# An explicit engine order for the QKV stage of a layernorm, linear-attention and SwiGLU kernel, with its weight sums moved to a later place

## The chip, the cores and the metric

The kernel runs on one core of one Trainium2 chip. Times are device microseconds (us) of one execution. The kernel was timed several times on the same chip beside the kernel that it is compared with; medians are given with the lowest and highest run. All runs used here are of the same (fast) state. The profile of a kernel is one execution, taken by the hardware profiler; its span is about 2 us shorter than the device time of the same execution.

Short names: PE is TensorE's matmul array, VectorE (DVE in the profile), ScalarE (ACT), GpSimd (POOL), SP the queue that issues most DMAs. The tiles in which the kernel collects PE's results (q_ps, kv_ps, nd_ps and others) are declared in PSUM, all its other tiles on the core in SBUF. L139 means line 139 of the kernel that is shown.

## The reference, cut to what matters

The input x is 2048 tokens by 1024. One normalized copy xn feeds a linear-attention block and a SwiGLU feed-forward, and the two results are combined.

```python
def phi(t): return where(t > 0, t + 1, exp(t)) + 1e-6
xn = layernorm(x)
q, k, v = split_heads(xn @ wqkv)          # 32 heads of 32
pq, pk = phi(q), phi(k)
kv  = einsum("bhsd,bhse->bhde", pk, v)    # sums over all 2048 tokens
z   = einsum("bhsd->bhd", pk)
num = einsum("bhqd,bhde->bhqe", pq, kv)
den = einsum("bhqd,bhd->bhq", pq, z)[..., None] + 1e-6
s   = (num / den) @ wo
g   = silu((silu(xn @ w_gate) * (xn @ w_up)) @ w_down)
out = x + s * g
```

Two consequences matter. The numerator (called ND below) needs kv of all tokens, so the kernel first runs k and v for all 16 token tiles (the QKV stage), then Q for a block of 512 tokens, then ND for that block. And the feed-forward is computed with a Winograd-like scheme on 2x2 blocks, for which sums of weight blocks (T1 to T4) are prepared on GpSimd while attention is still running.

## The kernel before

These are the parts that the change and the argument touch. Cuts are marked with "# ...".

The activation phi has two forms. Both are two VectorE steps after ScalarE's exponential; they differ in where the first step reads and writes:

```python
def emit_phi(work, t_ps, dst, W, in_place=False):
    e_t = work.tile([P, W], FP32, name="e_t", tag="e_t")
    ex = nc.scalar.activation(out=e_t[:], in_=t_ps, func=ACT.Exp)
    if in_place:                                   # first step stays in PSUM
        r = t_ps
        nc.vector.tensor_scalar(out=r, in0=t_ps, scalar1=0.0, scalar2=EPS, op0=ALU.max, op1=ALU.add)
    else:                                          # ScalarE copies to SBUF, first step SBUF to SBUF
        r_t = work.tile([P, W], FP32, name="r_t", tag="r_t")
        r = r_t[:]
        nc.scalar.activation(out=r, in_=t_ps, func=ACT.Relu)
        nc.vector.tensor_scalar(out=r, in0=r, scalar1=EPS, scalar2=None, op0=ALU.add)
    nc.vector.scalar_tensor_tensor(out=dst, in0=e_t[:], scalar=1.0, in1=r, op0=ALU.min, op1=ALU.add)
    return ex

def emit_Q(b, g):
    # ... eight matmuls into q_ps ...
    emit_phi(phiw, q_ps[:], pqT[:, g, :], TB)      # Q: the SBUF form, in both kernels
```

The weight sums: one set is four GpSimd sums and two DMA issues, also on GpSimd. prep takes the next of 14 sets from a queue: it loads a weight tile on SP and makes the sums.

```python
def emit_T(key, w):
    # ...
    nc.gpsimd.tensor_tensor(out=T1, in0=b12, in1=b11, op=ALU.subtract)
    nc.gpsimd.tensor_tensor(out=T2, in0=b22, in1=T1, op=ALU.subtract)
    nc.gpsimd.tensor_tensor(out=T3, in0=b22, in1=b12, op=ALU.subtract)
    nc.gpsimd.tensor_tensor(out=T4, in0=b21, in1=T2, op=ALU.subtract)
    # ... two nc.gpsimd.dma_start(...) that store T1..T4 in device memory

def prep(n, after=None):
    # ... t = w_slot(); load_gu(t, key[1], key[2], after); emit_T(key, t)
```

The QKV loop. The scheduler decides the order on each engine; the layernorm's Newton steps (reciprocal root by iteration), the norms and the copies of transposes are all VectorE's:

```python
for i in range(NT):                        # 16 token tiles
    ex = emit_B(i, 0)                      # k (c = 0, 1) and v (c = 2, 3) matmuls, phi in place
    # ...
    if i > 0:
        emit_C(i - 1)                      # kvz: pk^T [v, 1] of the tile before
    for c in range(1, NCH):
        if c == NCH // 2 and i + 2 >= TPB:
            stats_upto(i + 7)
        emit_B(i, c)
    if i >= 2 * TPB and i % 2 == 0:
        prep(1)                            # weight sums at tiles 8, 10, 12, 14
    nxt = i + 2
    if nxt < NPE:
        # ... emit_rstd (Newton steps) and emit_A2(nxt): norm, transposes, copy
    # ... for tiles 8 to 15: emit_rstd of four tiles, emit_A2_block: four norms (xn_blk),
    #     written to device memory on SP and read back transposed
# ...
gate(wq_loads, marks.get(("B", min(3, NT - 1))), sync=True)   # wq, wo: held until tile 3, tile 5
gate(wo_loads, marks.get(("B", min(5, NT - 1))), sync=True)
for g in range(G):
    emit_Q(0, g)
    if g % 4 == 3:
        prep(1)
```

The transposed attention output o of a block goes through device memory at once (emit_OT), and in the feed-forward the step c22 of the next key came after the matmuls and the evacuation of the present one:

```python
def emit_OT(b):
    # ...
    nc.sync.dma_start(out=blk_rows_pt(o_dram, b), in_=o_blk[:])
    nc.sync.dma_start_transpose(out=oT_tiles[b][:], in_=blk_rows(o_dram, b))
# ... feed-forward, for every key i:
    if i + 1 < n:
        emit_a(keys[i + 1])
    emit_b(keys[i])
    emit_evac(keys[i], h)
    if i + 1 < n:
        emit_c22(keys[i + 1])
```

Of the kernel before, what the change touches and what calls it, by code (L numbers as in the profile page):

```python
# [21 lines left out]
def kernel(  # L22
# [223 lines left out]
    with ExitStack() as p1:  # L246
# [5 lines left out]

        NXP = (NT + 1) // 2
# [32 lines left out]
        for i in range(nx, NT):  # L286
            load_x(i)
        wq_loads = [nc.gpsimd.dma_start(out=wq_sb[:, :, c * CW:(c + 1) * CW], in_=wqkv_v[:, :, c * CW:(c + 1) * CW])
                    for c in range(NCC)]
        wo_loads = [nc.gpsimd.dma_start(out=wo_sb[:, :, c * CW:(c + 1) * CW], in_=wo_v[:, :, c * CW:(c + 1) * CW])  # L290
                    for c in range(NCC)]

# [9 lines left out]
        def grp_of(i):  # L302
            return i if i < TPB else TPB - 1 + i // TPB

        def grp_tiles(gid):
            if gid < TPB:
                return [gid]
            b = gid - TPB + 1
            return list(range(b * TPB, min((b + 1) * TPB, NT)))

        def emit_stats(i):
            gid = grp_of(i)
            if gid not in grp_state:
                mv = small.tile([P, TPB, AGG], FP32, name="mv", tag="mv")
                rstd = small.tile([P, TPB], FP32, name="rstd", tag="rstd")
                grp_state[gid] = (mv, rstd, grp_tiles(gid))
            mv, rstd, tiles = grp_state[gid]
            k = tiles.index(i)
            stats = small.tile([P, NSC, nc.vector.BN_STATS_DIM], FP32, name="stats", tag="stats")
            xr = x_ap(i).rearrange("p (c f) -> p c f", f=SCH)  # L320
            sts = [nc.vector.bn_stats(out=stats[:, c, :], in_=xr[:, c, :]) for c in range(NSC)]  # L321
            if TPB <= i < 2 * TPB:
                late_gates.append((sts, ("B", min(1, NT - 1))))
            nc.vector.bn_aggr(out=mv[:, k, :], in_=stats[:])
            ln_state[i] = (mv, rstd, k)
            return sts
# [13 lines left out]
        def emit_rstd(gid):  # L340
            mv, rstd, tiles = grp_state[gid]
            n = len(tiles)
            a = small.tile([P, TPB], FP32, name="lna", tag="lna")
            nc.vector.tensor_scalar(out=a[:, 0:n], in0=mv[:, 0:n, 1], scalar1=EPS_LN, scalar2=None, op0=ALU.add)
# [5 lines left out]
            for _ in range(NR_ITERS):  # L350
                if n == 1:
                    nc.vector.scalar_tensor_tensor(out=w[:, 0:1], in0=y, scalar=a[:, 0:1], in1=y,
                                                   op0=ALU.mult, op1=ALU.mult)
                else:
                    nc.vector.tensor_tensor(out=w[:, 0:n], in0=y, in1=y, op=ALU.mult)
                    nc.vector.tensor_tensor(out=w[:, 0:n], in0=w[:, 0:n], in1=a[:, 0:n], op=ALU.mult)
                nc.vector.tensor_scalar(out=w[:, 0:n], in0=w[:, 0:n], scalar1=-0.5, scalar2=1.5,
                                        op0=ALU.mult, op1=ALU.add)
                nc.vector.tensor_tensor(out=y, in0=y, in1=w[:, 0:n], op=ALU.mult)
# [7 lines left out]
        def emit_A2(i):  # L367
            tok = slice(i * P, (i + 1) * P)
            xn = work.tile([P, D], BF16, name="xn", tag="xn")
            tr_ps = psC.tile([P, DC, P], BF16, name="tr_ps", tag="C")  # L370
            nh = 2 if (i == 0 and DC % 2 == 0) else 1
            dch = DC // nh
            cp = None
            for hh in range(nh):
                cols = slice(hh * dch * P, (hh + 1) * dch * P)
                emit_norm(i, xn[:, cols], cols=(cols if nh > 1 else None))
                for dc in range(hh * dch, (hh + 1) * dch):
                    nc.tensor.transpose(tr_ps[:, dc, :], xn[:, dc * P:(dc + 1) * P], ident[:])
                cp = nc.vector.tensor_copy(out=xn_ap(slice(hh * dch, (hh + 1) * dch), tok),
                                           in_=tr_ps[:, hh * dch:(hh + 1) * dch, :])  # L380
            ln_state.pop(i)
            return cp
# [11 lines left out]
        def emit_B(i, c):  # L394
            tok = slice(i * P, (i + 1) * P)
            if i not in pkv_tiles:
                pk_sb = work.tile([P, D], BF16, name="pk_sb", tag="pk_sb")
                pkv_tiles[i] = (pk_sb, v_bufs[i % 2])
            pk_sb, v_sb = pkv_tiles[i]
            kv_ps = psB.tile([P, CW], FP32, name="kv_ps", tag="B")  # L400
            for dc in range(DC):
                mm = nc.tensor.matmul(kv_ps[:], lhsT=xn_ap(dc, tok), rhs=wkv_sb[:, dc, c * CW:(c + 1) * CW],  # L402
                                      start=(dc == 0), stop=(dc == DC - 1))
                if dc == 0 and c == 0:
                    marks[("B", i)] = mm
            if c < NCC:
                return emit_phi(phiw, kv_ps[:], pk_sb[:, c * CW:(c + 1) * CW], CW, in_place=True)
            else:
                vc = c - NCC
                return nc.scalar.copy(out=v_sb[:, vc * GPC:(vc + 1) * GPC, 0:P],  # L410
                                      in_=kv_ps[:].rearrange("p (g c) -> p g c", c=P))
# [10 lines left out]
        nstat = 0  # L422

        def stats_upto(n):
            nonlocal nstat
            while nstat < min(n, NT):
                emit_stats(nstat)
                nstat += 1

        NPE = min(PE_T_BLOCKS * TPB, NT)  # L430
        cp0 = None
        sq_last = None
        for i in range(min(2, NT)):
            sts = emit_stats(i)
            nstat = i + 1
            if i > 0:
                gate(sts, cp0)
            sq_last = emit_rstd_act(grp_of(i))
            cp = emit_A2(i)
            if i == 0:  # L440
                cp0 = cp
        for i in range(NT):
            ex = emit_B(i, 0)
            if i == 0:
                gate([ex], sq_last)
            if i > 0:
                emit_C(i - 1)
            for c in range(1, NCH):
                if c == NCH // 2 and i + 2 >= TPB:
                    stats_upto(i + 7)  # L450
                emit_B(i, c)
            if i >= 2 * TPB and i % 2 == 0:
                prep(1)
            nxt = i + 2
            if nxt < NPE:
                if nxt < TPB:
                    stats_upto(nxt + 1)
                    emit_rstd(grp_of(nxt))
                elif nxt % TPB == 0:
                    stats_upto(nxt + TPB)  # L460
                    emit_rstd(grp_of(nxt))
                emit_A2(nxt)
            nb_ = (i + TPB) // TPB
            if (i + TPB) % TPB == 0 and nb_ >= PE_T_BLOCKS and nb_ < NB and i + TPB >= NPE:
                stats_upto((nb_ + 1) * TPB)
                emit_rstd(grp_of(nb_ * TPB))
                emit_A2_block(nb_)
        emit_C(NT - 1)
        gate([x_loads[i] for i in range(first_wave, NT)], marks.get(("B", min(1, NT - 1))), sync=True)
        for insts, key in late_gates:  # L470
            gate(insts, marks.get(key))
        gate(wq_loads, marks.get(("B", min(3, NT - 1))), sync=True)
        gate(wo_loads, marks.get(("B", min(5, NT - 1))), sync=True)
# [30 lines left out]
    with ExitStack() as p2:  # L504
# [36 lines left out]
        def emit_OT(b):  # L541
            oT_tiles[b] = otp.tile([P, G, TB], BF16, name="oT", tag="oT")
            o_blk = o_blks.pop(b)
            nc.sync.dma_start(out=blk_rows_pt(o_dram, b), in_=o_blk[:])
            nc.sync.dma_start_transpose(out=oT_tiles[b][:], in_=blk_rows(o_dram, b))
# [24 lines left out]
        for b in range(NB):  # L570
# [9 lines left out]
            for t in range(TPB):  # L580
                emit_ND(b, t)
                fill(1 if lastb else 2)
                if t % 2 == 1:
                    prep(1)
            emit_OT(b)
# [15 lines left out]
    with ExitStack() as p3:  # L601
# [35 lines left out]
        def emit_c22(key):  # L637
            p, kind, fg = key
            x_, zw, s2, s3, _ = grp[key]
            if kind == "g":  # L640
                c = xnp.tile([P, 4, TB], FP32, name="sg", tag="xn8")
                sg_tiles[(p, fg)] = c
            else:
                c = cp_.tile([P, 4, TB], FP32, name="cu", tag="cu")
            nc.vector.tensor_tensor(out=c[:, 3, :], in0=zw[:, 1, :], in1=s3[:], op=ALU.add)
            grp[key][4] = c

        def emit_b(key):
# [3 lines left out]
            x_, zw = grp[key][0:2]  # L652
            prod(zw[:, 0, :], lambda k: T4[:, k, :], lambda k: A22[:, k, :], False)
            prod(zw[:, 1, :], lambda k: w[:, HK + k, P:2 * P], lambda k: S4[:, k, :], False)
            prod(x_[:], lambda k: w[:, HK + k, 0:P], lambda k: x1[:, HK + k, :], False)

        def emit_evac(key, h):
            p, kind, fg = key
            x_, zw, s2, s3, c = grp.pop(key)
            nc.vector.tensor_tensor(out=c[:, 1:3, :], in0=zw[:], in1=s2[:, None, :].to_broadcast([P, 2, TB]),  # L660
                                    op=ALU.add)
            if kind == "g":
                nc.scalar.activation(out=c[:, 1:4, :], in_=c[:, 1:4, :], func=ACT.Silu)  # L663
# [9 lines left out]
        NRES = 5  # L673

        def emit_down(p, sw, h, w0, last):
# [17 lines left out]
            for q in range(NQ - NRES):  # L693
                load_w_to(w0 + q + 6)
                for t in range(TPB):
# [29 lines left out]
        with tc.manual_schedule(engines={mybir.EngineType.PE, mybir.EngineType.DVE, mybir.EngineType.Activation,  # L725
                                         mybir.EngineType.Pool}):
            base = 0
            for pi, p in enumerate(passes):
# [17 lines left out]
                for i in range(n):  # L746
# [5 lines left out]
                    emit_b(keys[i])  # L752
                    emit_evac(keys[i], h)
                    if i + 1 < n:
                        emit_c22(keys[i + 1])
# [38 lines left out]
```

## Time and profile before

| what | value | which view |
|---|---|---|
| time | 828.19 us (827.65 to 829.03, 3 runs) | runs |
| span, PE busy | 825.6 us, 96% | page, part 1 |
| PE idle before the first transpose | 6.2 us | PE waits |
| longest wait of PE inside the QKV stage | 8.9 us, for VectorE's pk | PE waits |
| last kvz matmul, first nd_ps, first yb (feed-forward) | 147.2, 164.1, 266.3 us | PE timeline |
| GpSimd's sums | 1.15 us each, 48.5 to 149.8 us | GpSimd timeline |

PE is busy 96% of the span, so only its idle stretches can be won. The page shows the span in 40 slices of 20.6 us; a digit is the busy share in tenths, and PEclk is the granted clock of TensorE in tenths of full speed:

```profile
PE   5976999999999999999999999999999999999997
...
PEclk9997999999999999999999999999999999999999
```

The third and fourth slices (41 to 83 us) have PE at 7 and 6, and the clock is at 7 in the fourth. The PE's waits (columns: total us, times, longest) name the cause:

```profile
PE kv_ps L402 <- DVE pk_sb L140: 8.9, 1, 8.9
PE tr_ps L378 <- DVE xn L364: 6.7, 3, 6.2
PE zw L613 <- DVE cu L645: 2.2, 2, 1.1
PE s_ps L555 <- DMA oT<-o_dram: 1.5, 1, 1.5
```

A kv matmul waits 8.9 us for pk, a VectorE result. (6.2 of the 6.7 us of the second line are the start.) The windows of the core show how busy the engines were; in each line: us, then busy us and instructions of PE, weight loads, VectorE, ScalarE and GpSimd, then clock and DMA:

```profile
40.00:60.00 20.00, 17.68 (x110) 8.96 (x108) 20.00 (x49) 5.36 (x10) 11.36 (x12) 1.00 0.64 205
60.00:80.00 20.00, 11.88 (x57) 5.73 (x57) 15.21 (x28) 2.37 (x4) 9.08 (x11) 0.74 1.06 323
...
140.00:160.00 20.00, 19.99 (x106) 9.47 (x104) 11.17 (x22) 9.75 (x18) 10.88 (x13) 1.00 0.50 200
160.00:180.00 20.00, 20.00 (x121) 10.19 (x120) 18.29 (x57) 11.08 (x21) 0.00 (x0) 1.00 0.00 1
```

VectorE is full from 40 to 60 us and PE loses 8 us of the next 20. Why VectorE is late is seen only in its timeline. VectorE first (start us, us, line, operation):

```profile
53.70 3.99 DVE L359 TENSOR_TENSOR rstd<-rstd,lnw 128x4 f32<-128x4 f32 x1
...
61.69 3.98 DVE L364 TENSOR_SCALAR xn_blk<-xp,mv,rstd 128x1024 bf16<-128x1024 bf16 x1
```

A step that multiplies 128x4 numbers, L359, takes 3.99 us (usual: 0.15), and a norm, L364, takes 3.98 us (usual: 0.54). GpSimd in the same stretch:

```profile
54.27 1.17 POOL L212 TENSOR_TENSOR T_1055<-w_sb 128x512 fp32r<-128x512 bf16 x1
55.39 1.15 POOL L214 TENSOR_TENSOR T_1056<-w_sb 128x512 fp32r<-128x512 bf16 x1
56.50 1.15 POOL L213 TENSOR_TENSOR T_1055<-w_sb,T_1055 128x512 fp32r<-128x512 bf16 x1
...
62.00 1.16 POOL L212 TENSOR_TENSOR T_1177<-w_sb 128x512 fp32r<-128x512 bf16 x1
```

L359 starts at 53.70, while GpSimd issues a DMA, and ends at 57.69, when the three sums from 54.27 on have ended (the last one at 57.65); the norm of 61.69 ends at 65.67, after the three sums that begin at 62.00. So the sums seem to hold VectorE.

Q's two VectorE steps of before; the sums ended at 149.8 us, just before the first of them:

```profile
149.89 0.43 DVE L139 TENSOR_SCALAR r_t<-r_t 128x512 f32<-128x512 f32 x1 [1.54 <-ACT r_t L138]
150.35 0.69 DVE L140 SCALAR_TENSOR_TENSOR pqT<-e_t,r_t 128x512 bf16<-128x512 f32 x1
...
152.08 0.69 DVE L140 SCALAR_TENSOR_TENSOR pqT<-e_t,r_t 128x512 bf16<-128x512 f32 x1
```

### The profile page before, as it was taken

What the parts mean: (1) busy time and instruction counts of PE and PEld (TensorE: products, weight loads), DVE (VectorE), ACT (ScalarE), POOL (GpSimd) and SP (SyncE); (2) the same over time, 40 slices, a digit from 0 to 9 for tenths busy, and PEclk for the clock granted to TensorE, in tenths of its full rate; (3) what the DMA queues carried; (4) which work ended last, traced back from release to release, by engine and by line L of the source; (5) the groups of instructions that cost most, each with busy time, mean ns of one, the idle gap of its engine ahead of it and who ended that gap; (6) DMA issues with size and microseconds to landing.
All of it is one profiled execution on the core that took longest, in us unless ns stands there. A gap on an engine that the chain in (4) does not pass through costs nothing.

```text
span 825.6 us, 9966 instructions
## 1 busy us (share of the span) xinstructions
PE 794.9 (96%) x3808; PEld 431.9 (52%) x3808; DVE 465.7 (56%) x787; ACT 202.9 (25%) x312; POOL 185.3 (22%) x221
## 2 busy tenths in 40 slices
PE   5976999999999999999999999999999999999997
PEld 2443444454454666666664444456666666544443
DVE  7996343695753666767665044166676676611305
ACT  2221333554533222122221021022212212200102
POOL 0064799300011253443650010010000000000100
PEclk9997999999999999999999999999999999999999
DMA  9469998217343678778687448389777777753641
GB/s 305 159 208 330 320 336 326 105 52 185 98 156 111 193 232 268 236 235 273 206 296 240 153 131 314 122 255 348 236 257 254 247 233 264 261 169 127 226 150 52
DMA packets 149566, 178.91 MB, mean 217 GB/s; under 512 B 30736, under 2 KB 105872, under 8 KB 149520
## 3 DMA queue, kind: packets, MB, share of 16 engines
q1 hardware_dynamic: 137792, 137.25, 52.0%
q0 software_dynamic: 11584, 40.90, 14.0%
q8 instruction: 30, 0.49, 0.2%
q10 hardware_dynamic: 144, 0.13, 0.0%
q14 instruction: 16, 0.13, 0.0%
HBM read 127.93 MB, written 44.04 MB: 208 GB/s over the span
## 4 chain that ended last, share of the span: by engine, by line
PE 88%; DVE 8%; DMA 3%; SPq 0%; issue 0%; ACT 0%; ACTq 0%
PE zw L613 24%; PE y_pd L690 12%; PE xb L613 11%; PE y_ps L690 11%; PE kv_ps L402 9%; PE q_ps L157 7%; PE s_ps L555 6%; PE yb L613 6%; DVE stats L321 2%; DMA xp<-in_A_x_dram 1%; PE nd_ps L527 1%; DVE xn_blk L364 1%; DVE kv_ps L134 1%; DMA oT<-o_dram 1%; DMA w_sb<-in_B_w_up_dram 1%; DMA w_sb<-in_B_w_down_dram 1%
## 5 line engine op out<-in xcount | busy, mean ns | idle before, releaser
L690 PEld LDWEIGHTS <-hT 128*128 128x128 bf16 x896 | 87.7, 98 | 107.3 <-issue 1.7
L402 PE MATMUL kv_ps<-wkv_sb,xnT 128*128 128x512 bf16 x512 | 117.8, 387 | 10.2 <-DVE pk_sb L140 8.9
L613 PE MATMUL xb<-xnT,w_sb 128*128 128x512 bf16 x448 | 115.5, 380 | 0.4 <-DMA w_sb<-in_B_w_up_dram 0.4
L690 PE MATMUL y_pd<-w_sb,hT 128*128 128x512 bf16 x448 | 103.2, 379 | 1.4 <-DMA w_sb<-in_B_w_down_dram 1.4
L690 PE MATMUL y_ps<-w_sb,hT 128*128 128x512 bf16 x448 | 103.2, 379 | 0.0
L720 DVE TENSOR_TENSOR sy<-sy,io 128x512 f32<-128x512 f32 (+1 forms) x33 | 22.2, 673 | 140.1 <-ACT sy L719 140.1
L613 PEld LDWEIGHTS <-w_sb 128*128 128x128 bf16 x672 | 56.8, 98 | 83.7 <-issue 30.2
L723 POOL DMA_DIRECT2D out_dram<-io x24 | 13.0, 543 | 337.8 <-DVE io L721 337.8
L402 PEld LDWEIGHTS <-xnT 128*128 128x128 bf16 x512 | 50.1, 100 | 68.3 <-issue 14.0
L663 ACT ACTIVATE sg<-sg 128x1536 f32<-128x1536 f32 x28 | 41.6, 1486 | 122.7 <-DVE sg L660 122.7
L555 PE MATMUL s_ps<-wo_sb,oT 128*128 128x512 bf16 x256 | 56.6, 379 | 1.5 <-DMA oT<-o_dram 1.5
L157 PE MATMUL q_ps<-xnT,wq_sb 128*128 128x512 bf16 x256 | 57.2, 379 | 0.0
L669 DVE TENSOR_TENSOR hT<-cu,sg 128x1536 bf16<-128x1536 f32 x28 | 49.9, 1781 | 0.0
L719 ACT ACTIVATE sy<-y_pd 128x512 f32<-128x512 f32 x16 | 8.7, 594 | 156.3 <-PE y_pd L690 156.3
L134 DVE TENSOR_SCALAR kv_ps<-kv_ps 128x512 f32<-128x512 f32 x32 | 22.3, 699 | 42.8 <-ACT e_t L131 42.7
L555 PEld LDWEIGHTS <-oT 128*128 128x128 bf16 x256 | 24.7, 98 | 30.6 <-DMA oT<-o_dram 2.0
L157 PEld LDWEIGHTS <-wq_sb 128*128 128x128 bf16 x256 | 24.6, 98 | 27.4
L560 POOL DMA_DIRECT2D s_dram<-s_sb x16 | 8.7, 543 | 108.5 <-ACT s_sb L557 108.5
L131 ACT ACTIVATE e_t<-kv_ps 128x512 f32<-128x512 f32 x32 | 19.1, 597 | 47.7 <-PE kv_ps L402 30.3
L613 PE MATMUL zw<-S_4505,w_sb 128*128 128x512 f16 x112 | 29.0, 382 | 0.0
L613 PE MATMUL zw<-S_2588,w_sb 128*128 128x512 f16 x112 | 29.0, 382 | 0.0
L557 ACT CAST s_sb<-s_ps 128x512 bf16<-128x512 f32 x32 | 18.8, 586 | 38.2 <-PE s_ps L555 37.6
(970 smaller groups left out, 1181.9 us busy)
## 6 DMA issues: line engine op xcount, KB each, us to landing
w_sb<-in_B_w_down_dram SPq DMA_DIRECT2D x56, 512.0 KB, 3.6
w_sb<-in_B_w_gate_dram SPq DMA_DIRECT2D x40, 512.0 KB, 4.8
w_sb<-in_B_w_up_dram SPq DMA_DIRECT2D x28, 512.0 KB, 6.1
o_dram<-o_blk SPq DMA_DIRECT2D x4, 1024.0 KB, 4.4
s_dram<-s_sb POOLq DMA_DIRECT2D x16, 256.0 KB, 2.7
io<-in_A_x_dram SPq DMA_DIRECT2D x16, 256.0 KB, 3.1
io<-s_dram SPq DMA_DIRECT2D x16, 256.0 KB, 3.4
xp<-in_A_x_dram SPq DMA_DIRECT2D x15, 256.0 KB, 6.4
```

The lines of the kernel that those rows point to most:

```text
L131: ex = nc.scalar.activation(out=e_t[:], in_=t_ps, func=ACT.Exp)
L134: nc.vector.tensor_scalar(out=r, in0=t_ps, scalar1=0.0, scalar2=EPS, op0=ALU.max, op1=ALU.add)
L157: nc.tensor.matmul(q_ps[:], lhsT=wq_sb[:, dc, g * P:(g + 1) * P], rhs=xn_ap(dc, btok), start=(dc == 0), stop=(dc == DC - 1))
L321: sts = [nc.vector.bn_stats(out=stats[:, c, :], in_=xr[:, c, :]) for c in range(NSC)]
L402: mm = nc.tensor.matmul(kv_ps[:], lhsT=xn_ap(dc, tok), rhs=wkv_sb[:, dc, c * CW:(c + 1) * CW], start=(dc == 0), stop=(dc == DC - 1))
L555: nc.tensor.matmul(s_ps[:], lhsT=oT[:, c, ttok], rhs=wo_sb[:, c, cc * CW:(cc + 1) * CW], start=(c == 0), stop=(c == G - 1))
L557: nc.scalar.copy(out=s_sb[:, cc * CW:(cc + 1) * CW], in_=s_ps[:])
L613: nc.tensor.matmul(out, lhsT=lhs(k), rhs=rhs(k), start=(first and k == 0), stop=(k == HK - 1), skip_group_check=True)
L663: nc.scalar.activation(out=c[:, 1:4, :], in_=c[:, 1:4, :], func=ACT.Silu)
L669: nc.vector.tensor_tensor(out=hv[:, TB:4 * TB], in0=c[:, 1:4, :].rearrange("p a b -> p (a b)"), in1=sg[:, 1:4, :].rearrange("p a b -> p (a ...
L690: nc.tensor.matmul(ys[(t, c)], lhsT=h[:, fc, tt], rhs=wt[:, o:o + CW], start=(fc == 0), stop=(fc == FC - 1), skip_group_check=True)
L720: nc.vector.tensor_tensor(out=sy[:], in0=sy[:], in1=s_in[:, cs], op=ALU.mult)
```

## The change

The intent is to remove the hole of PE in the QKV stage by taking work off VectorE and by moving the sums out of its way, and to remove some small waits later. In the QKV stage every engine's order is now written by hand: tiles 0 and 1 use each weight chunk together, layernorm runs two tiles ahead, the Newton steps go to GpSimd, the copies of the transposes go to ScalarE from tile 2 on, and sums are asked for only from tile 10 on. For tiles 0 to 8, k's phi takes the SBUF form. Later: o is transposed in halves, c22 (one VectorE add on a key's products) comes ahead of the matmuls of the present key, the SiLU is done in more, smaller steps, and the down projection begins with three weight tiles at once. The core of the diff:

```diff
+        p1_man = ExitStack()
+        p1_man.enter_context(tc.manual_schedule(engines={PE, DVE, Activation, Pool, SP}))   # cut
-        wq_loads = [nc.gpsimd.dma_start(...)]           # cut: gated until tile 3
-        wo_loads = [nc.gpsimd.dma_start(...)]           # cut: gated until tile 5
         def emit_rstd(gid):
+            eng = nc.gpsimd
-            nc.vector.tensor_scalar(out=a[:, 0:n], in0=mv[:, 0:n, 1], scalar1=EPS_LN, ...)
+            eng.tensor_scalar(out=a[:, 0:n], in0=mv[:, 0:n, 1], scalar1=EPS_LN, ...)
             for _ in range(NR_ITERS):
+                eng.tensor_tensor(out=w[:, 0:n], in0=y, in1=y, op=ALU.mult)
+                eng.tensor_tensor(out=w[:, 0:n], in0=w[:, 0:n], in1=a[:, 0:n], op=ALU.mult)
+                eng.tensor_scalar(out=w[:, 0:n], in0=w[:, 0:n], scalar1=-0.5, scalar2=1.5, ...)
+                eng.tensor_tensor(out=y, in0=y, in1=w[:, 0:n], op=ALU.mult)
# ... emit_TR: the copy of the transposes
+                if i < 2:
+                    nc.vector.tensor_copy(out=dst, in_=tr_ps[:])
+                else:
+                    nc.scalar.copy(out=dst, in_=tr_ps[:])
# ... emit_Bev
-                return emit_phi(phiw, kv_ps[:], pk_sb[:, c * CW:(c + 1) * CW], CW, in_place=True)
+                emit_phi(phiw, kv_ps[:], pk_sb[:, c * CW:(c + 1) * CW], CW, in_place=i >= 9)
# ... the order of tiles 0 and 1 by hand, then the loop:
+        for i in range(2, NT):
+            for c in range(NCH):
+                emit_Bmm(i, c)
+                # ... TR(i + 1), C(i - 1), Bev(i, c), N(i + 2), layernorm of i + 3
+            if i == 3 or i == 5:       # wq, wo loads: by program order in GpSimd's queue
+                # ... nc.gpsimd.dma_start(...)
+            if i >= 10:
                 prep(1)
# ... emit_OT(b, hf): half a block at a time; feed-forward:
                     if i + 1 < n:
                         emit_a(keys[i + 1])
-                    emit_b(keys[i])
+                        emit_c22(keys[i + 1])
+                    emit_b(keys[i], i == n - 1)
                     emit_evac(keys[i], h)
-                    if i + 1 < n:
-                        emit_c22(keys[i + 1])
# ... SiLU of c22 apart from the rest; NRES 5 -> 4; QF = 3 tiles of the down projection first
```

## The prediction

> **What bounds the kernel now.** PE is busy 96% of the 825.6 us span (page, busy table), so only PE's idle stretches can be won. The stretches and the table of waits show: 6.2 us before the first transpose; 8.9 us at 59-68 us, where a kv matmul waits for VectorE's pk; shorter waits of 0.4-0.8 us before and between; 1.5 us for the last transposed o; in the feed-forward stage 2.2+0.7 us of zw waiting for cu/sg and 1.8 us for weights; a 5 us tail. The QKV stage ends at 147.4 us, though its warm pace (7.37 us per tile, chain of waits) would need about 121 us. The 9 us hole also drops the granted clock to 0.5 (64-72 us).
>
> Why VectorE was late: it is 100% busy from 20 to 68 us (windows), and from 49 us GpSimd's weight sums (1.15 us each) hold it up: one rstd step took 3.99 us instead of 0.15, one norm 3.98 instead of 0.5, each ending with a run of three sums (timeline). [...]
>
> **What the change does in the QKV stage.** Newton steps (about 12 small operations per group, 0.15-0.2 us) go to GpSimd, transpose copies (0.68 us) to ScalarE; weight sums start only after the last block norm. Tiles 0 and 1 share weight chunks. I expect no PE hole over 2 us: first matmuls at the same 6-7 us, stage end near 132 us (7.7 + 16x7.37 + 7 transposes x 0.45[...]), so 13-16 us won.
>
> **What it costs: the main doubt.** In before, GpSimd's sums end at 149.8 us, just before the first Q evacuation. In after, the first weight load for a sum stands on the DMA queue behind the last block's transpose; I estimate the first sum at about 86 us. Fifteen sets at 5.65 us each (trace) end near 170 us, so 35 us of them fall on Q (from 132 us). Q's evacuation is r_t (0.43 us, SBUF to SBUF) and a two-input step on two SBUF tensors (0.69 us): both kinds collide. If VectorE passes only in the gaps between runs, it finishes one Q per about 5 us instead of 1.73. ND needs all eight, so PE then stalls up to 10-24 us.
>
> **Elsewhere.** Half-block o transposes remove the 1.5 us wait; c22 ahead of evacuation removes about 2.9 us of zw waits; NRES/QF up to 1 us: 4-5 us won.
>
> **Sum.** 828 - 15 (QKV) - 4.5 (elsewhere) + 16 (Q, between 2 and 24): 825 us, range 808-836. Within 2%, unless the collision is mild.
>
> **What would show it.** Right: windows 20-70 with PE full; granted clock 1.0 there; QKV ends 130-134 us; in the Q stretch r_t and pqT instructions of 2-5 us against 0.43/0.69, PE idle waiting for them until the sums end, and the first nd_ps later than 160 us (before: 164.1). Wrong: r_t stays at 0.43 us on average and first nd_ps near 148 us: then about 809 us.
>
> **What would make it wrong.** The sums run at another time; [...] small GpSimd Newton steps are much slower than on VectorE (0.2 us) and delay norms in tiles 2-7; VectorE falls behind.
>
> Chances: faster by over 2%: 0.2; within 2%: 0.76; slower by over 2%: 0.04.

Cut from it is a term of 2 us in the sum for the end of the QKV stage: with it the sum came to 130.8 us ("near 132"), the terms that remain give 128.8 us. What the trace of before shows is that the first 13 kv matmuls, from 7.72 us on, took 4.70 us and 11 of them from 13.64 us on 2.54 us, with the clock at 1.00 from 0 to 20 us; what slowed the first ones isn't shown. The "warm pace" is that of the undisturbed tiles of before, 7.37 us each (kv matmuls from 82.05, 89.42 and 96.79 us on), with the clock at 1.00. "Both kinds collide" rests on the two steps of before shown above: L359, with two SBUF inputs, took 3.99 instead of 0.15 us, and the norm L364, from SBUF to SBUF, 3.98 instead of 0.54 us.

## The result, and the profile after

The changed kernel took 829.65 us (829.32 to 830.66, 4 runs); before, on the same chip, took 828.07 us (827.65 to 829.03, 4 runs). The ratio is 1.002, with a 95% interval of 1.0002 to 1.0037: the same within 2%. Here and below a ratio is the mean time of one kernel's fast runs over the mean of the other's of the same rounds, so it is not quite the ratio of the medians that are quoted.

The same parts of the page for the changed kernel (slices of 20.7 us):

```profile
PE   6999999579999999999999999999999999999997
...
PEclk9999999769999999999999999999999999999999
```

The hole of the third and fourth slices is gone, and a new one is in the eighth and ninth (145 to 186 us), with the clock at 7 and 6. PE's waits:

```profile
PE q_ps L157 <- ACT r_t L138: 9.6, 4, 4.8
PE tr_ps L384 <- DVE xn L360: 8.4, 3, 6.0
PE nd_ps L552 <- DVE pqT L140: 5.3, 2, 2.8
PE kv_ps L408 <- DMA xnT<-xn_dram: 1.5, 1, 1.5
```

No wait for pk, cu, w_down or oT is left. In their place Q's matmuls wait 9.6 us for ScalarE's r_t, and ND waits 5.3 us for pqT. ScalarE is not the origin: it waits itself for VectorE's pqT, 26.0 us in eight times, because r_t and e_t have two buffers each. The windows:

```profile
40.00:60.00 20.00, 18.33 (x108) 9.22 (x109) 13.96 (x34) 9.11 (x15) 13.80 (x42) 1.00 0.35 114
60.00:80.00 20.00, 18.44 (x107) 9.23 (x110) 13.17 (x28) 9.50 (x17) 5.20 (x15) 1.00 0.96 255
...
140.00:160.00 20.00, 13.27 (x46) 5.11 (x46) 19.90 (x8) 4.34 (x8) 19.94 (x22) 0.77 0.84 291
160.00:180.00 20.00, 11.56 (x45) 4.88 (x44) 18.48 (x27) 6.12 (x12) 13.27 (x15) 0.63 0.60 234
```

PE wins 6.6 us in 60 to 80 us (18.44 against 11.88) and loses 6.7 and 8.4 us in the two windows after 140 us. VectorE is busy 19.90 of 20 us with only 8 instructions. Four of them in a row:

```profile
140.13 3.83 DVE L139 TENSOR_SCALAR r_t<-r_t 128x512 f32<-128x512 f32 x1
144.00 0.69 DVE L140 SCALAR_TENSOR_TENSOR pqT<-e_t,r_t 128x512 bf16<-128x512 f32 x1
144.61 6.03 DVE L139 TENSOR_SCALAR r_t<-r_t 128x512 f32<-128x512 f32 x1
150.67 0.69 DVE L140 SCALAR_TENSOR_TENSOR pqT<-e_t,r_t 128x512 bf16<-128x512 f32 x1
```

with GpSimd beside them:

```profile
142.52 1.15 POOL L215 TENSOR_TENSOR T_1899<-w_sb,T_1898 128x512 fp32r<-128x512 bf16 x1
143.62 0.57 POOL L220 DMA_DIRECT2D t_g_1904<-T_1898  x1
144.19 0.53 POOL L220 DMA_DIRECT2D t_g_1905<-T_1899  x1
144.75 1.17 POOL L212 TENSOR_TENSOR T_1910<-w_sb 128x512 fp32r<-128x512 bf16 x1
```

The r_t of 140.13 takes 3.83 us instead of 0.43 and ends at 143.96, after the last sum of a run of three; pqT then passes in 0.69 us inside the two DMA issues (143.62 to 144.72). The next r_t starts at 144.61, 0.14 us before the next sum, and is held for five sums, until 150.64. Only in the last set of sums (167.0 to 172.3 us) does VectorE pass after each sum, with steps of 1.4 to 1.6 us. There the second sum starts 0.08 us after the first has ended (168.24 after 168.16); in the runs of sums that held VectorE, each sum starts just within the end of the one before (by 0.03 to 0.06 us in the change). In the kept traces of all kernels, a waiting r_t, pqT or block norm passed at all five boundaries between two sums that have such a gap; of 83 boundaries without one it passed at 12, at 11 of them right after it had passed at the boundary before (in the change alone: at the one with a gap, and at 2 of 17 without, at 169.4 and 171.0 us). That fits the gap as what lets VectorE in, but no run tested it, and in before_late_sums VectorE also passed after each of five sums between 137.8 and 144.6 us, which leave no such gap. So, before the last set, one Q passes per set of DMA issues: from 139.53 to 166.25 the pqT steps begin 4.5 or 6.7 us apart, 5.3 us on average, where before took 1.73. Over the whole kernel the step L139 reads (min/median/max ns):

```profile
L139 DVE TENSOR_SCALAR r_t<-r_t x50: 374/427/6028, 14.2 to 233.9; 128x512 f32<-128x512 f32 x50
```

PE meanwhile:

```profile
166.30 0.99 PE L552 MATMUL nd_ps<-KVZ,pqT 128*128 128x132 bf16 x6
...
172.93 0.29 PE L552 MATMUL nd_ps<-KVZ,pqT 128*128 128x132 bf16 x1 [2.57 <-DVE pqT L140]
173.02 4.47 PE L157 MATMUL q_ps<-xnT,wq_sb 128*128 128x512 bf16 x10
```

The first nd_ps is issued at 166.30 but its group of eight is complete only at 172.93, when the sums have ended too (172.3 us).

Adding up the profiled spans (825.6 and 828.0): the last kvz matmul ends 12.2 us earlier (147.4 to 135.2). From there to Q's first matmul after the first ND group takes 37.8 us instead of 17.1 us: 20.7 us lost. From there to the first yb of the feed-forward it is 102.7 against 101.8 us: 0.9 us lost. The feed-forward from its first yb takes 552.3 instead of 559.3 us: 7.0 us won. The sum is -12.2 + 20.7 + 0.9 - 7.0 = +2.4 us, the difference of the spans. Everything that was won is given back in one place.

### The profile page after: what moved, and what is told of

Same layout as the page of the kernel before. It is cut to its first block, busy times and chain, and to the rows that moved or that the text cites. A ratio compares the mean times of both kernels' runs of the same rounds, so it can differ in the third digit from the quotient of the medians.

```text
span 828.0 us, 10023 instructions
## 1 busy us (share of the span) xinstructions
PE 794.4 (96%) x3736; PEld 434.3 (52%) x3808; DVE 475.1 (57%) x728; ACT 221.5 (27%) x364; POOL 214.4 (26%) x325
## 4 chain that ended last, share of the span: by engine, by line
PE 87%; DVE 7%; DMA 3%; POOL 2%; issue 1%; ACT 1%; DVEq 0%; ACTq 0%
PE zw L641 25%; PE xb L641 12%; PE y_pd L726 11%; PE y_ps L726 11%; PE kv_ps L408 9%; PE s_ps L583 7%; PE yb L641 6%; PE q_ps L157 5%; DVE r_t L139 3%; DMA xnT<-xn_dram 1%; DMA xn_dram<-xn_blk 1%; PE nd_ps L552 1%; DVE pqT L140 1%; DVE sy L763 0%; DVE stats L322 0%
## 5 line engine op out<-in xcount | busy, mean ns | idle before, releaser
L408 PE MATMUL kv_ps<-wkv_sb,xnT 128*128 128x512 bf16 x499 | 114.3, 383 | 2.1 <-DMA xnT<-xn_dram 1.5
L641 PE MATMUL xb<-xnT,w_sb 128*128 128x512 bf16 x420 | 113.7, 380 | 1.5
L157 PE MATMUL q_ps<-xnT,wq_sb 128*128 128x512 bf16 x250 | 64.2, 410 | 10.1 <-ACT r_t L138 9.6
L698 ACT ACTIVATE sg<-sg 128x1024 f32<-128x1024 f32 x28 | 29.6, 1058 | 97.1 <-DVE sg L694 97.1
L139 DVE TENSOR_SCALAR r_t<-r_t 128x512 f32<-128x512 f32 x50 | 46.0, 920 | 15.4 <-ACT r_t L138 15.1
L131 ACT ACTIVATE e_t<-q_ps 128x512 f32<-128x512 f32 x32 | 19.1, 597 | 50.2 <-DVE pqT L140 26.0
```

The lines of the kernel that those rows point to most:

```text
L157: nc.tensor.matmul(q_ps[:], lhsT=wq_sb[:, dc, g * P:(g + 1) * P], rhs=xn_ap(dc, btok), start=(dc == 0), stop=(dc == DC - 1))
L408: mm = nc.tensor.matmul(kv_ps[:], lhsT=xn_ap(dc, tok), rhs=wkv_sb[:, dc, c * CW:(c + 1) * CW], start=(dc == 0), stop=(dc == DC - 1))
L641: nc.tensor.matmul(out, lhsT=lhs(k), rhs=rhs(k), start=(first and k == 0), stop=(k == HK - 1), skip_group_check=True)
L698: nc.scalar.activation(out=c[:, 1:3, :], in_=c[:, 1:3, :], func=ACT.Silu)
```

## The experiments

The theory: the sums, now later, run through Q's evacuation, whose two VectorE steps are of the two kinds that were held beside the sums in before (two SBUF inputs: L359, 3.99 us; SBUF to SBUF: L364, 3.98 us); this, and nothing else in the change, costs some 20 us. Rivals: (A) ScalarE's two steps per Q, or the two buffers, are too slow; (B) the explicit order itself delays the Q stage; (C) only r_t, the step from SBUF to SBUF with one tensor in, collides, not pqT. Later the question was also which part of the change wins the QKV stage. In the expectations "Theory" means the theory given here.

A table of all runs first, for reference; "last kvz" and the rest are start times in the profiled run. Times are medians.

| kernel | time us | ratio to before | last kvz | first nd_ps | first yb |
|---|---|---|---|---|---|
| before | 828.07 | 1 | 147.2 | 164.1 | 266.3 |
| the change | 829.65 | 1.0020 | 135.0 | 166.3 | 275.7 |
| q_inplace | 809.96 | 0.9781 | 137.3 | 154.2 | 255.3 |
| q_onestep | 807.56 | 0.9759 | 137.2 | 154.1 | 254.6 |
| few_sums | 808.19 | 0.9762 | 137.5 | 154.4 | 254.9 |
| q_twoin | 827.16 | 0.9993 | 137.1 | 168.1 | 273.9 |
| late_only | 820.72 | 0.9912 | 148.0 | 164.9 | 265.4 |
| qkv_only | 837.65 | 1.0112 | 135.0 | 166.6 | 276.4 |
| before_late_sums | 849.34 | 1.0258 | 135.9 | 161.4 | 288.7 |
| newton_dve_q1 | 827.33 | 0.9984 | 154.2 | 171.1 | 271.6 |
| newton_dve_gated | 817.03 | 0.9867 | 144.3 | 161.2 | 261.7 |
| before_late_onestep | 844.36 | 1.0228 | 136.9 | 153.8 | 283.6 |
| onestep_all | 804.76 | 0.9721 | 132.7 | 149.6 | 250.2 |
| before_late_free | 823.49 | 0.9941 | 139.9 | 156.8 | 265.3 |

The kernel before had medians of 828.33, 828.88, 827.76 and 827.67 us in the four batches. The same QKV code ended at 135.0 us in two runs and near 137.3 in four others, so 2 us of the column "last kvz" are spread between runs.

### q_inplace: Q's first step stays in PSUM

The changed kernel with one word more:

```diff
-        emit_phi(phiw, q_ps[:], pqT[:, g, :], TB)
+        emit_phi(phiw, q_ps[:], pqT[:, g, :], TB, in_place=b < 2)
```

> The changed kernel, with one edit: the Q evacuation of blocks 0 and 1 works in place in PSUM (ScalarE exp only; VectorE max-and-add PSUM to PSUM, then a step with one PSUM and one SBUF input)[...]. Theory [...]: the 20 us stall of the Q stretch vanishes, VectorE's steps stay at 0.7 us each beside the running sums, the first complete group of nd_ps ends near 153 us instead of 173 us, total 805 to 811 us. Rival A (ScalarE's two activations per Q limit it, since PE's waits name r_t on ScalarE): also faster, as ScalarE has one activation less. Rival B (the new order or DMA traffic of the sums stalls it): no change, 828 to 831 us.

Measured: 809.96 us, ratio 0.9781 (0.9762 to 0.9800). The sums run on through this stretch as in the change (GpSimd busy 19.94 of 20 us in 140 to 160), with the same DMA traffic (289 GB/s, the last figure; 291 in the change), and PE is full (20.00 of 20). The window, and then the first step of those Qs (min/median/max ns):

```profile
140.00:160.00 20.00, 20.00 (x106) 9.63 (x105) 17.23 (x34) 6.57 (x11) 19.94 (x22) 1.00 0.85 289
L134 DVE TENSOR_SCALAR q_ps<-q_ps x16: 672/699/700, 139.6 to 167.9; 128x512 f32<-128x512 f32 x16
```

The first step now takes 0.70 us and pqT at most 0.69 us. So VectorE does the same number of steps, even slower ones by name (0.70 instead of 0.43 us), and the stall of 20 us is gone. What counts here is which memory a step works on beside GpSimd's sums (at most 0.70 us for a step with a tensor in PSUM, up to 6.03 us for r_t in the change), not how much VectorE has to do.

### q_onestep: one VectorE step, still two on ScalarE

```diff
+    def emit_phi1(work, t_ps, dst, W):
+        e_t = work.tile([P, W], FP32, name="e_t", tag="e_t")
+        nc.scalar.activation(out=e_t[:], in_=t_ps, func=ACT.Relu, scale=-1.0)    # max(-x, 0)
+        nc.scalar.activation(out=e_t[:], in_=e_t[:], func=ACT.Exp, scale=-1.0)   # min(exp(x), 1)
+        nc.vector.scalar_tensor_tensor(out=dst, in0=t_ps, scalar=EPS, in1=e_t[:],
+                                       op0=ALU.max, op1=ALU.add)                 # max(x, eps) + e_t
-        emit_phi(phiw, q_ps[:], pqT[:, g, :], TB)
+        emit_phi1(phiw, q_ps[:], pqT[:, g, :], TB)
```

(For x above 1e-6 this leaves out the added 1e-6; the result stays correct within the comparison's tolerance.)

> The changed kernel, with Q's evacuation written as ScalarE relu(-x), ScalarE exp(-that), and one VectorE step max(q, eps) + e with one PSUM and one SBUF input. ScalarE keeps two activations per Q[...]. Theory [...]: stall gone, first complete nd_ps group near 153 us, total 803 to 809 us, and a little better than q_inplace because VectorE has 0.7 us of work per Q instead of 1.4. Rival A (ScalarE is the limit): unchanged near 829 us, ScalarE having as much to do as before. Rival B: unchanged.

Measured: 807.56 us, ratio 0.9759 (0.9740 to 0.9778). All 32 evacuations take the same time, although the sums go on to 172.7 us:

```profile
L148 DVE SCALAR_TENSOR_TENSOR pqT<-q_ps,e_t x32: 691/692/693, 140.1 to 213.0; 128x512 bf16<-128x512 f32 x32
```

ScalarE still does two activations per Q here, and PE does not wait for it: rival A falls. The step reads one tensor from PSUM and one from SBUF; it isn't touched by the sums (691 to 693 ns beside them and after them).

### few_sums: half the sums ahead

```diff
-    NPREP = 12
+    NPREP = 6
```

> The changed kernel with NPREP 6 instead of 12: 9 sets of sums before the feed-forward stage instead of 15; the others are made in its first pass. Theory [...]: sums end near 140 us instead of 173 us, so only about 5 us of them fall on the Q stretch; r_t back to 0.43 us after that; Q resumes at 155 to 160 us. The total is open, because six more sets now run in the first pass of the feed-forward stage, where VectorE has a two-SBUF-input step of 1.8 us per pair: 810 to 828 us. Rivals A and B (ScalarE, order): the Q stretch stays as it is, Q resumes near 173 us.

Measured: 808.19 us, ratio 0.9762 (0.9740 to 0.9785). The sums end near 139.8 us, Q's code is unchanged, and the first nd_ps comes at 154.4 us. In the window 140 to 160 GpSimd is busy 0.81 us and PE 20.00:

```profile
140.00:160.00 20.00, 20.00 (x106) 9.59 (x105) 14.78 (x36) 12.13 (x23) 0.81 (x2) 1.00 0.14 53
```

Taking the sums away works as well as taking the collision away, so the explicit order itself does not delay Q: rival B falls. The total lies just below the 810 to 828 us that were expected: the six sets that are now made in the feed-forward cost nothing there (from first yb to the end 553.0 us, 553.2 in q_onestep).

### q_twoin: only the step with two SBUF inputs

```diff
             nc.scalar.activation(out=r, in_=t_ps, func=ACT.Relu)
-            nc.vector.tensor_scalar(out=r, in0=r, scalar1=EPS, scalar2=None, op0=ALU.add)
+            if W != TB or not q_stage:        # q_stage: set for Q alone; Q loses its 1e-6
+                nc.vector.tensor_scalar(out=r, in0=r, scalar1=EPS, scalar2=None, op0=ALU.add)
```

> The changed kernel with VectorE's r_t step left out in the Q stretch (the eps of 1e-6 is not added; the result changes by less than rounding). What stays is the step with two SBUF inputs, 0.69 us[...]. If two SBUF inputs collide with the sums [...]: the pqT step waits in r_t's place, lasting 2 to 6 us beside the sums, one or two Qs pass per gap; Q resumes between 158 and 172 us, total 812 to 828 us. [...] pqT stays at 0.69 us, total 804 to 809 us.

(The second case, pqT at 0.69 us, is that of rival C.)

Measured: 827.16 us, ratio 0.9993 (0.9962 to 1.0025). Nothing is won. Nine pqT steps in a row, merged in one line of VectorE's timeline (start, us):

```profile
139.78 33.84 DVE L141 SCALAR_TENSOR_TENSOR pqT<-e_t,r_t 128x512 bf16<-128x512 f32 x9 [1.54 <-ACT r_t L138]
```

That is 3.8 us each instead of 0.69, with a longest of 6.74 us. So a step with two SBUF inputs collides by itself, without any r_t step near it: rival C falls. Taking one of two colliding steps away wins nothing: in the changed kernel one long and one short step passed per gap of GpSimd, here one long step. The first three took 12.91 us (139.78 to 152.69), and in them GpSimd had three such gaps, the DMA issues from 140.98, 145.43 and 152.10 us on (1.10 us each).

### late_only and qkv_only: the two halves of the change

late_only is the kernel before with only the later edits (halved o transposes, feed-forward); qkv_only is before with only the QKV part:

```diff
# late_only: QKV stage of before, with
+        def emit_OT(b, hf): ...
+                        emit_c22(keys[i + 1])     # ahead of emit_b
# qkv_only: the explicit QKV stage, everything after Q as in before
```

> Only the later part of the change: half-block o transposes and the feed-forward edits, on the QKV stage of before. The traces of before and after say 6.1 us of feed-forward time and 1.5 us of waiting for the transposed o: total 820 to 823 us.

> Only the QKV part of the change, on the later stages of before. Theory: QKV stage about 12 us shorter, Q stretch 20 to 21 us longer, later stages as before: total 835 to 838 us, over 0.8% slower than before. If the later edits have no worth of their own: 829 to 831 us.

Measured: late_only 820.72 us, ratio 0.9912 (0.9883 to 0.9942), with the hole of before (9.1 us of waiting for pk). qkv_only 837.65 us, ratio 1.0112 (1.0087 to 1.0137), with the new waits (11.3 us for r_t, 5.3 us for pqT) and the old later ones. By medians of the same batch, -8.2 and +8.8 us; they add up to +0.6 us where the whole change is +1.6. So the later edits are worth 8 us and the QKV part as it stands loses 9 us.

### before_late_sums: only the place of the sums

The kernel before, not its order, with the sums later and their loads held tile by tile:

```diff
-            if i >= 2 * TPB and i % 2 == 0:
-                prep(1)
+            if i >= 10:
+                prep(1, after=marks.get(("B", i)))
```

> The kernel before, with one edit: its weight sums start with token tile 10 (one set per tile, each load gated by the tile's first matmul), about where the changed kernel has them. Nothing else of the change. Theory [...]: the 8.9 us hole at 59-68 us closes, because the norms no longer meet the sums, and the QKV stage ends 8 to 12 us earlier, near 136 to 140 us; the stall of 15 to 21 us appears in the Q stretch instead, with r_t of 2 to 6 us; total 830 to 838 us. Rival (the stall is a work of the new engine order, the hole one of VectorE's load): the hole stays, no stall in the Q stretch, total 826 to 830 us.

Measured: 849.34 us, ratio 1.0258 (1.0227 to 1.0289). The hole at 60 us is gone and the last kvz starts at 135.9 us, 11.3 us earlier than in before, with the same work on VectorE and still in an order that the scheduler chose. The window that had PE at 11.88 us in before:

```profile
60.00:80.00 20.00, 19.89 (x116) 10.04 (x116) 9.45 (x16) 5.92 (x10) 0.00 (x0) 1.00 0.87 238
```

So the hole came from the sums' place, and most of the QKV gain (12.2 us) can be had without the explicit order. The stall then appears in Q and ND: 9.9 us for pqT, 8.9 us for o_blk, 6.7 us for r_t. The total was expected at 830 to 838 us and missed, because the loads were held one per tile: the sums began at 96.5 and ended only at 194.9 us, so they also met the first ND.

### newton_dve_q1 and newton_dve_gated: Newton steps back on VectorE

Both are q_onestep with the Newton steps on VectorE. In the second one the wq and wo loads are also held until tiles 3 and 5, as in before.

```diff
         def emit_rstd(gid):
-            eng = nc.gpsimd
+            eng = nc.vector
# newton_dve_gated also:
-                    nc.gpsimd.dma_start(out=wt[...], in_=wv[...])
+                    d = nc.gpsimd.dma_start(out=wt[...], in_=wv[...])
+                    gate([d], marks.get(("B", i)), sync=True)
```

> As q_onestep (807.6 us), with the Newton steps back on VectorE, in the new order. If moving them to GpSimd is worth something, tiles 2 to 7 show more waits of transposes for xn (1.5 to 2.5 us now), by up to 13 steps of 0.2 us in line per group: 808 to 814 us. If GpSimd's slower steps (0.27 us from one to the next, 0.65 us where they meet VectorE) cost as much: 806 to 808 us.

> newton_dve_q1 was no clean test: with the Newton steps off GpSimd nothing held back the loads of wq and wo on its queue, they were issued at 1.4 us, and a kv matmul waited 8.9 us for its weights. Here those loads wait for the first matmul of tiles 3 and 5. What is left is the Newton steps' own cost: expected no wait for weights in the first 25 us; transposes waiting for xn by 4 to 8 us beyond the first one (4.6 us at tile 7 in newton_dve_q1, 2.5 us with the steps on GpSimd); total 809 to 815 us against 807.6 for q_onestep. If the steps cost nothing in line: 806 to 809 us.

newton_dve_q1 measured 827.33 us, ratio 0.9984 (0.9954 to 1.0015), but it didn't test what it was made for. With no Newton steps in GpSimd's queue nothing stands ahead of the wq and wo loads: they were issued at 1.4 to 5.5 us, and PE then waited 8.9 us for the k and v weights that it needs first, a wait that q_onestep does not have:

```profile
PE kv_ps L415 <- DMA wkv_sb<-in_A_wqkv_dram: 8.9, 1, 8.9
```

This is a lesson in itself: in the changed kernel's order the small steps on GpSimd also act as the gate of four loads of 1 MB (in q_onestep, with the same order, issued at 52.1 and 60.1 us). newton_dve_gated removes that, and measured 817.03 us, ratio 0.9867 (0.9843 to 0.9892):

```profile
PE tr_ps L391 <- DVE xn L367: 15.4, 4, 5.9
```

5.9 us of this is the start; the other 9.5 us are transposes waiting for norms that q_onestep has 3.2 us of (9.3 less 6.1). Against q_onestep the Newton steps on GpSimd are worth 9.5 us by medians (817.03 less 807.56, from two batches; the kernel came out above the 809 to 815 us expected). In the two profiled runs it is 7.0 us, all of it in the QKV stage (last kvz at 144.3 against 137.2). The test is not quite of the Newton steps alone: here the loads of wq and wo were issued at 39.2 and 54.8 us, in q_onestep at 52.1 and 60.1. On GpSimd the steps follow each other by 0.28 us (on VectorE by 0.19), and last up to 0.72 us where they meet VectorE (in the change the one of 46.99 us, beside VectorE's pk step from 46.95 to 47.64 us); with layernorm two tiles ahead, the total is 7.0 to 9.5 us lower all the same.

### before_late_onestep: late sums and one-step Q in the kernel before

```diff
# before_late_sums, and in emit_Q:
-        emit_phi(phiw, q_ps[:], pqT[:, g, :], TB)
+        emit_phi1(phiw, q_ps[:], pqT[:, g, :], TB)
```

> The kernel before with two edits only: late sums as in before_late_sums, and Q's evacuation in one VectorE step as in q_onestep. No explicit order, no shared weight chunks, Newton steps on VectorE. Theory: the sums meet neither the norms nor Q; the QKV stage ends near 136 us as in before_late_sums, the Q stretch takes its 17 us as in before: 11 us below before, 815 to 819 us. If the explicit order is what shortens the QKV stage, it stays near 147 us: 826 to 829 us.

Measured: 844.36 us, ratio 1.0228 (1.0179 to 1.0277); the expectation is missed by 25 us. Q and ND do run without a stall (first nd_ps at 153.8, before: 164.1). The loss is in another place:

```profile
PE s_ps L562 <- DMA oT<-o_dram: 24.8, 2, 18.6
```

The o of a block is written by SP, in the program behind weight loads for the sums. The queue's timeline shows that the write came only right after such a load (start, us, line):

```profile
177.84 0.37 SPq L188 DMA_DIRECT2D w_sb<-in_B_w_up_dram  x1
178.30 0.53 SPq L551 DMA_DIRECT2D o_dram<-o_blk  x1
```

The o of block 0 was finished on VectorE at 169.0 us (its twelfth o_blk step), but written only at 178.30, and read back transposed from 187.17 on; PE got it at 200.5 us, after its longest wait of 18.6 us. Ahead of the write stood a weight load for a sum set, issued at 177.84 us: the queue's waits show these loads waiting 41.9 us in nine times for GpSimd's T, because a load needs a weight buffer that the sums give free. The sums, paced one set per tile from 97.25 us, ended only at 193.6 us. So late sums do harm a second time, through the DMA queue that they share with o.

### onestep_all: the one-step form for k too

```diff
# q_onestep, and in emit_Bev:
-                emit_phi(phiw, kv_ps[:], pk_sb[:, c * CW:(c + 1) * CW], CW, in_place=i >= 9)
+                emit_phi1(phiw, kv_ps[:], pk_sb[:, c * CW:(c + 1) * CW], CW)
```

> Candidate for the best: the changed kernel with the one-step evacuation for k as well as for Q, which takes 0.43 us per evacuation from VectorE in tiles 0 to 8 and 0.7 us from there on. Expected: transposes wait 1 to 2 us less for xn, the block norms come earlier, so the wait for the transposed block (2 to 2.8 us) shrinks: 803 to 808 us. If VectorE was not what those waits hang on: 807 to 809 us.

Measured: 804.76 us (804.28 to 806.08, 5 runs), ratio 0.9721 (0.9700 to 0.9743). It beats both kernels. PE is busy 98% of its span. Its waits:

```profile
PE tr_ps L391 <- DVE xn L367: 6.2, 1, 6.2
PE kv_ps L415 <- DMA xnT<-xn_dram: 1.2, 1, 1.2
PE kv_ps L415 <- DVE pk_sb L148: 0.4, 1, 0.4
```

After the start, PE waits 1.6 us in all, and the last kvz starts at 132.7 us. All 64 evacuations of k and Q took 680 to 693 ns, 30 of them beside sums.

### before_late_free: the same as before_late_onestep, without the pacing

```diff
+            if i >= 10:
+                prep(1, after=marks.get(("B", 8)))
```

> Kernel before with the sums emitted from tile 10 on, their loads all held only until the first matmul of tile 8 (about 77 us) instead of one per tile, and the one-step Q evacuation. It asks whether late sums and the one-step Q are enough without the explicit engine order and without the later edits. My theory (the sums' place on VectorE's path is what made the hole, and the slow late sums of before_late_onestep were only its pacing): sums run back to back from about 83-90 us to about 170-175 us, QKV ends at 134-138 us, the first nd_ps at about 153 us, the wait of s_ps for the transposed o at most 5 us, total 814-822 us (ratio 0.983-0.993). Rival (the explicit order carries a good part of the gain itself, since unpaced sums meet the VectorE work of tiles 8-15 in the scheduler's order): a PE hole of over 3 us reappears after 83 us, QKV ends after 140 us, total over 823 us. Also possible: the scheduler pulls the sums before the block norms again (sums start near 78 us but VectorE stalls), which would show as rstd or norm steps of over 2 us.

Measured: 823.49 us (822.25 to 826.65, 4 runs), ratio 0.9941 (0.9918 to 0.9965). It lies above my 814 to 822 and meets the rival's total of over 823; the last kvz starts at 139.9 us (7.3 us earlier than in before, but expected at 134 to 138), the first nd_ps at 156.8 us (7.3 us earlier). The rival's hole isn't there: in every window of 20 us from 60 to 240 us PE is busy 19.84 us or more, with the sums running from 89.1 us on. The late end of QKV doesn't speak for the rival either. The profiled execution is the longest of the four (826.65 us); its clock was 0.50 in 16 to 20 us (0.86 over 0 to 20 us), where before_late_onestep had 1.00, and the 3.0 us by which its last kvz comes later than there (136.9) are lost before 26 us, before any sum. From there on the unpaced sums cost QKV nothing, and the long wait of before_late_onestep for o is gone, so the pacing was indeed its fault. But PE then waits 6.2 us for the last transposed o (before: 1.5 us). VectorE's timeline shows why:

```profile
232.97 0.15 DVE L539 TENSOR_SCALAR rden<-nd_ps 128x8 f32<-128x8 f32 x1
233.04 2.28 DVE L504 TENSOR_TENSOR S<-xnT 128x2048 fp32r<-128x2048 bf16 x1
...
237.56 0.42 DVE L542 TENSOR_TENSOR o_blk<-nd_ps,rden 128x256 bf16<-128x256 f32 x1
```

The scheduler put two sums of the feed-forward (S, 2.28 us each) between the last steps that make o_blk: one at 233.04, one at 235.35 us. The o write was issued at 238.01 us, only 3.1 us earlier than in before (241.13), although the last nd_ps came 7.3 us earlier. This is not the price of the missing explicit order: that order ends before Q in the changed kernel too, and onestep_all has the same two sums (225.89 and 228.21 us) ahead of its last o_blk step, without any wait for o. What onestep_all has and this kernel lacks is, among the later edits, the halved o transposes; this kernel was not run with them.

## Why the prediction was right

It was right in the time (825 predicted, 829.65 measured, inside 808 to 836) and in the class, and its two big terms had the right cause. Luck helped with the total: the range for Q (2 to 24 us lost) was so wide that most outcomes would have fallen inside, the net was forecast as 3.5 us won and came out as 1.6 us lost, and the misses partly cancelled (by the profiles QKV won 2.8 us less and Q lost 4.7 us more than forecast, the rest won 1.6 us more). Point by point:

- **The hole came from the sums.** Right. before_late_sums removes it by moving the sums alone.
- **QKV: 15 us won (13 to 16).** 12.2 us measured, just short of the range. PE's hole over 2 us is gone from this stage as predicted, but it ended at 135.2 us, not 130 to 134: three small waits remained (xn 0.9 and 1.6 us, the transposed block's DMA 1.5 us). onestep_all, which relieves VectorE further, gets rid of most of them; its last kvz starts at 132.7 us instead of 135.0.
- **Q: 16 us lost (2 to 24).** 20.7 us measured, of the predicted cause. "r_t of 2 to 5 us" was right in kind; the longest lasted 6.03 us, beside a run of five sums. "One Q per about 5 us" was 5.3 us. The first nd_ps came "later than 160 us", at 166.3. The estimate for the sums was good: start predicted at 86, measured 88.2 us; end predicted near 170, measured 172.3 us.
- **Both kinds of step collide.** Right. q_twoin shows it for two SBUF inputs alone (up to 6.74 us). The other kind was seen in the trace of the change, not in a run of its own: r_t has one SBUF tensor in and one out, and took 0.43 us without the sums and up to 6.03 us beside them; the similar step in PSUM (q_inplace) took 0.70 us beside them. The multiplication by 128x4 numbers that took 3.99 us in before has two SBUF inputs.
- **Elsewhere: 4.5 us won (4 to 5).** Undersized. late_only wins 8.2 us by medians; in the profile of the change the feed-forward alone is 7.0 us shorter, of which the listed waits that vanished are 4.7 us (zw 2.9, weights 1.8). The other 2.3 us have no line in the table of waits, and I didn't settle them.
- **The clock.** The prediction counted the clock in the QKV hole but not in the new one: PE was granted 0.77 in 140 to 160 and 0.63 in 160 to 180 us. It has hardly a share in the 4.7 us by which the Q term was too small: from the first r_t (137.69) to the end of the eighth pqT (172.88) VectorE is busy 34.91 of 35.19 us, so it almost never waited for a Q that a slow PE had delayed. The clock was still 0.50 just after, from 173.0 to 177.5 us, in the stretch that lost 0.9 us.
- **"Small GpSimd Newton steps could delay norms."** They did not do harm; in newton_dve_gated, with the steps back on VectorE, 7.0 us (profiles) to 9.5 us (medians) were lost in this order.
- **What the prediction credited to the order is partly the sums'.** 7.3 us (before_late_free, whose profiled execution had lost 3.0 us at the start) to 11.3 us (before_late_sums) of the 12.2 us come with the scheduler's own order and late sums. What the order and the Newton steps add of their own was not separated: the two before_late kernels with a one-step Q lose at the transfer of o, and both lack the later edits. As an estimate, q_onestep is 15.9 us below before_late_free, and the later edits alone were worth 8.2 us in late_only, so some 8 us or less are left for the order and the Newton steps together.

In both profiles the granted clock was lower in and after PE's longest stalls. In before it read 0.80 in 60 to 64 us, 0.50 in 64 to 72 us, in and right after the hole, and 0.92 in 72 to 76 us; in the change 1.00 up to 150 us, 0.59 in 150 to 155 and 0.50 in 155 to 160 us.

## What to carry to other kernels

When background work on GpSimd is moved in time, look at what VectorE does in its new place. Here a step from SBUF to SBUF took up to 6.03 us instead of 0.43 (r_t) and one that reads two SBUF tensors up to 6.74 us instead of 0.69 (q_twoin), each for a run of GpSimd's sums, while the form with one tensor from PSUM was not touched (691 to 693 ns in q_onestep), and changing that form was worth 20 us, more than any change of order. Moving work also moves what stands in the queues: in before_late_onestep a load that waited for late sums held the write of o behind it, from 169.0 to 178.30 us, and in newton_dve_q1, without the small steps in GpSimd's queue, loads started at 1.4 us instead of 52.1.
